# A small weight load moved from sixteen DMA engines to four

The last 64 rows of one weight matrix (72 KB of the 88.5 MB that the kernel loads) were loaded by all sixteen DMA engines. The change loads them by one transfer that only DMA engines 0 to 3 carry.

## The chip, the cores and the metric

One core of one Trainium2 chip. Times are device microseconds (us) of single executions, as medians of several. A ratio compares the fast runs of two kernels in the same rounds on the same chip and is given with its 95% interval, so it isn't quite the ratio of the medians. A run is fast when it lies within 1.5% of the fastest run of the same kernel. Landings and packet times come from one profiled execution of each kernel and are counted from the start of its span (the time from the first to the last instruction of the profile). The packet records carry no engine number: "engines 0 to 3" is the name of the four DMA engines that carried the four packets of x (a load of 4 rows). In profile lines PE is the matmul engine, PEld its weight loads, DVE, ACT and POOL are VectorE, ScalarE and GpSimd, SP is SyncE; a q behind a name marks what its sequencer does, such as issuing a load. L176 is line 176 of the kernel.

## The reference, cut to what matters

One decode step: attention over the last 2048 positions of a cache beside an MLP, both fed by a layer norm of x.

```python
xn = _layernorm(x)                       # x: 4 x 576
return x + _A_ref(xn, k_cache, v_cache, wq, wo) + _B_ref(xn, w1, w2, w3, w4)
...
def _B_ref(x, w1, w2, w3, w4):           # w1, w2: 576 x 576
    h = _gelu(_layernorm(x) @ w1)
    hs = shifted(h) @ w2                 # cut: four groups of columns, shifted
    x1 = x + hs
    return x1 + _gelu(_layernorm(x1) @ w3) @ w4
```

There are 4 rows of activations, so nearly all the work is to read the K and V windows and the weights once from memory.

## The kernel before

576 rows are 4 x 128 + 64. The first 512 rows of each weight go to 128 partitions. The 64 rows that are left (the "rag") are paired: one matrix takes the even partitions of a tile, another the odd ones, and the transposed activations hold zeros where the other matrix lies, so that one matmul over 128 partitions uses one of the two.

```python
def rag_pair(tile, even, odd):
    return [(tile[p:128:2, 0:w.shape[1]], w[512:576, :]) for p, w in enumerate((even, odd))]
...
ev_wq = [add_dma([(kt_t[:], A_wq[0:512, :]...)], "wq", (), -60),             # 4 MB
         add_dma(rag_pair(ragq3, B_w3, A_wq), "wqr", ["ragq3_zero"], -59)]
ev_r12 = add_dma(rag_pair(rag12, B_w1, B_w2), "r12", (), -58.5)             # the rag of w1 and w2
ev_w2 = add_dma([(w2main, ...)], "w2", (), -58)
ev_w1 = add_dma([(w1main, ...)], "w1", (), -57)
... # w3, sixteen K blocks of 2 MB, sixteen V blocks, wo, w4
def pe_h(h):
    def f(e):
        for r in range(4):
            e.matmul(HTps[h], lhsT=xn2T[:, r, :], rhs=w1main[:, r, ...], start=(r == 0), stop=False)
        return e.matmul(HTps[h], lhsT=xn2T[:, 4, :], rhs=rag12[:, ...], start=False, stop=True)
```

All loads but that of x are issued by SyncE on one queue, in this order.

## Time and profile before

| | before |
|---|---|
| time, median of 6 runs | 215.06 us (214.81 to 215.25) |
| span of the profiled execution | 213.7 us |
| loads of the kernel | 88.5 MB, 97.7% of the sixteen engines' span |
| last landing of a load | 211.48 us |
| that landing, engine by engine | spread over 2.15 us |

The first row is from the runs, the next two are from the page of the profile. The kernel is bound by its DMA engines (first packet 1.85 us, the DMA row at 9 in all slices between the first and the last). How the lines of this profile are read is shown in the prediction below.

### The profile page before, as it was taken

What the parts mean: (1) busy time and instruction counts of PE and PEld (TensorE: products, weight loads), DVE (VectorE), ACT (ScalarE), POOL (GpSimd) and SP (SyncE); (2) the same over time, 40 slices, a digit from 0 to 9 for tenths busy, and PEclk for the clock granted to TensorE, in tenths of its full rate; (3) what the DMA queues carried; (4) which work ended last, traced back from release to release, by engine and by line L of the source; (5) the groups of instructions that cost most, each with busy time, mean ns of one, the idle gap of its engine ahead of it and who ended that gap; (6) DMA issues with size and microseconds to landing.
All of it is one profiled execution on the core that took longest, in us unless ns stands there. A gap on an engine that the chain in (4) does not pass through costs nothing. (4 is left out here: it accounts for less than half of the span.)

```text
span 213.7 us, 5906 instructions
## 1 busy us (share of the span) xinstructions
PE 141.4 (66%) x2664; PEld 110.4 (52%) x2668; DVE 75.3 (35%) x147; ACT 61.2 (29%) x76; POOL 10.8 (5%) x38
## 2 busy tenths in 40 slices
PE   0038683999999999999996277133444433336995
PEld 0023363788878887888774067033434433334542
DVE  0142511477776676666664830100010001001000
ACT  2001032366655666666656620000000000000000
POOL 8300100000001000000000000000000000000000
PEclk9999999799999999999999655555555555555799
DMA  7999999999999999999999999999999999999993
GB/s 282 406 385 449 438 411 442 414 429 422 432 426 429 429 423 435 422 432 420 439 423 432 420 425 427 427 426 435 426 423 426 429 429 426 429 429 436 426 404 124
DMA packets 6690, 88.65 MB, mean 415 GB/s; under 512 B 780, under 2 KB 1048, under 8 KB 1560
## 3 DMA queue, kind: packets, MB, share of 16 engines
q1 hardware_dynamic: 6664, 88.50, 97.7%
q8 instruction: 8, 0.13, 0.2%
q14 instruction: 2, 0.02, 0.0%
q10 hardware_dynamic: 16, 0.01, 0.0%
HBM read 88.49 MB, written 0.00 MB: 414 GB/s over the span
## 5 line engine op out<-in xcount | busy, mean ns | idle before, releaser
L336 PE MATMUL ps<-perm_bf,ring 128*128 128x128 bf16 x1024 | 62.5, 221 | 3.0 <-PEq L575 2.4
L336 PEld LDWEIGHTS ps<-perm_bf,ring 128*128 128x128 bf16 x1024 | 58.3, 98 | 11.3 <-issue 11.1
L343 DVE COPY kt<-ps 128x1024 bf16<-128x1024 bf16 x80 | 52.4, 688 | 28.5 <-PE ps L336 28.0
L342 ACT ACTIVATE kt<-ps 128x1024 bf16<-128x1024 bf16 x48 | 48.4, 1023 | 33.0 <-PE ps L336 32.3
L417 PE MATMUL ps<-PTpad,ring 128*128 128x8 bf16 x1024 | 29.7, 168 | 41.5 <-PEq L575 37.5
L417 PEld LDWEIGHTS ps<-PTpad,ring 128*128 128x128 bf16 x1024 | 28.7, 104 | 42.6 <-issue 42.5
L552 ACT ACTIVATE out_sb<-ps 4x288 bf16<-4x288 f32 x1 | 0.4, 401 | 87.5 <-PE ps L434 87.5
L350 PE MATMUL ps<-kt,Qs 128*32 128x512 bf16 x272 | 18.5, 393 | 1.4 <-PEq L575 1.4
L406 DVE TENSOR_TENSOR PTpad<-PT,mU_bf 128x512 bf16<-128x512 bf16 x16 | 6.4, 421 | 29.7 <-PE ps L417 29.7
L429 DVE TENSOR_TENSOR OTn<-ps,rinvB 128x32 bf16<-128x32 f32 x4 | 0.8, 192 | 34.5 <-PE ps L417 34.5
L277 PE MATMUL ps<-ident_bf,xn_bf 4*128 4x4 bf16 x8 | 0.5, 170 | 13.9 <-DVE ragsrc L271 13.9
L350 PEld LDWEIGHTS ps<-kt,Qs 128*32 128x32 bf16 x272 | 5.9, 98 | 7.2 <-issue 2.2
L371 POOL COPY Qs<-Qpad 128x128 bf16<-128x128 bf16 x16 | 4.6, 293 | 86.8 <-PE ps L350 72.5
L277 PEld LDWEIGHTS ps<-ident_bf,xn_bf 4*128 4x128 bf16 x8 | 0.4, 111 | 14.0 <-issue 11.6
L434 PE MATMUL ps<-w,ORT 128*4 128x288 bf16 x64 | 5.8, 358 | 0.4 <-DVE ORT L456 0.4
L551 DVE CAST out_sb<-ps 4x288 bf16<-4x288 f32 x1 | 0.4, 446 | 14.5 <-PE ps L434 14.5
L434 PE MATMUL ps<-w,h2T_sb 128*4 128x288 bf16 x72 | 5.0, 286 | 0.4 <-DMA w<-in_B_w_dram 0.4
L264 ACT ACTIVATE sd<-mv 4x1 f32<-4x1 f32 x3 | 0.6, 202 | 15.8 <-DVE mv L262 15.8
L388 PE MATMUL ps<-kt,permT_bf 128*128 128x512 bf16 x3 | 1.8, 608 | 4.9 <-DVE kt L387 4.8
L434 PEld LDWEIGHTS ps<-w,ORT 128*4 128x4 bf16 x64 | 3.4, 106 | 3.0 <-DVE ORT L456 1.0
L434 PEld LDWEIGHTS ps<-w,h2T_sb 128*4 128x4 bf16 x72 | 2.9, 84 | 2.8 <-DMA w<-in_B_w_dram 1.8
L440 PE MATMUL ps<-zeros_bf 128*128 128x512 bf16 x13 | 3.8, 419 | 0.4 <-DVE OTn L429 0.2
(99 smaller groups left out, 65.9 us busy)
## 6 DMA issues: line engine op xcount, KB each, us to landing
ring<-in_A_k_cache_dram SPq DMA_DIRECT2D x16, 2048.0 KB, 14.4
ring<-in_A_v_cache_dram SPq DMA_DIRECT2D x16, 2048.0 KB, 17.4
w<-in_B_w_dram SPq DMA_DIRECT2D x2, 2304.0 KB, 21.9
w<-in_A_wo_dram SPq DMA_DIRECT2D x2, 2304.0 KB, 21.1
kt<-in_A_wq_dram SPq DMA_DIRECT2D x1, 4096.0 KB, 12.3
w<-in_B_w_dram SPq DMA_DIRECT2D x1, 2592.0 KB, 28.1
w<-in_B_w_dram SPq DMA_DIRECT2D x3, 576.0 KB, 13.6
w<-in_B_w_dram SPq DMA_DIRECT2D x1, 1296.0 KB, 30.7
```

Source lines behind the costliest of these rows:

```text
L277: e.transpose(XTps[idx][:, r, :], v[:, r, :], ident_bf[0:B, 0:B])
L336: ins = e.transpose(tb[n % 4][:, t, :], slot_t(c)[:, 8 * k + t, :], perm_bf[:])
L342: return "act", lambda e: e.activation(out=ktbuf[:, n % 16], in_=tb[n % 4], func=ACTF.Copy)
L343: return "dve", lambda e: e.tensor_copy(out=ktbuf[:, n % 16], in_=tb[n % 4])
L350: ins = e.matmul(Sps[32 * u:32 * u + 32, q, :].rearrange("p (t i) -> p t i", t=16), lhsT=Qs[:, c % NPOS, 32 * u:32 * u + 32], rhs=ktgrp[:, ...
L371: P(lambda e, c=c, cc=cc: e.tensor_copy(out=Qs[:, c % NPOS, :], in_=Qpad_t[:, 128 * cc:128 * cc + 128]), waits=["qT", "qs_zero"] + ([f"SC{ ...
L388: add("pe", lambda e, q=q: e.matmul(ps[:, 4 + q % 3, :], lhsT=permT_bf[:], rhs=PTx[:, q, :], start=True, stop=True), waits=[f"PTx{q}", "pe ...
L406: return lambda e: e.tensor_tensor(out=PTpad[:, c % 2], in0=PTv[:, :, cc, :].unsqueeze(2).to_broadcast([128, NT, NU, 2]), in1=mU_bf[:].uns ...
L417: ins = e.matmul(o_, lhsT=slot_t(c)[:, t, :], rhs=PTpad[:, c % 2, t].rearrange("p u e -> p (u e)"), start=(t == 0), stop=(t == NT - 1))
L429: add("dve", lambda e, hv=hv: e.tensor_tensor(out=hv(OTn), in0=OTps.rearrange("p (b h) -> p b h", b=B), in1=hv(rinvB), op=ALU.mult), waits ...
L434: return e.matmul(ACC[h], lhsT=lhsT, rhs=rhs, start=start, stop=stop, tile_position=(0, 32 * h), skip_group_check=True)
L440: ins = e.matmul(ps[:, 3, :], lhsT=zeros_bf[:, 0:128], rhs=zeros_bf[:, :], start=True, stop=True)
```

## The change

Intent: engines 0 to 3 finish early, so give them the whole of this load and take its share from the other twelve. The new transfer has outermost dimensions 16 (partitions) on one side and 4 (groups of rows) on the other. Four rows of w1 go side by side into one partition, so the rag becomes 16 partitions of 4 x 576 numbers, and its one matmul becomes four of 16 rows each.

```diff
+        w1rag = w4_t[0:16, 18 * D:22 * D]
...
+        P(lambda e: e.memset(rag12[:], 0.0), sig="rag12_zero", key=-98)
...
-        ev_r12 = add_dma(rag_pair(rag12, B_w1, B_w2), "r12", (), -58.5)
+        ev_r12 = add_dma([(w1rag, B_w1[512:576, :].rearrange("(b a c) n -> a b (c n)", b=4, a=4)),
+                          (rag12[1:128:2, :], B_w2[512:576, :])], "r12", ["rag12_zero"], -58.5)
...  # the columns of the normed x in the matching order (one copy)
+                for c in range(4):
+                    ins = e.transpose(XTps[idx][0:16, 4 + c, :], ragsrc[:, idx, 16 * c:16 * c + 16], ident_bf[0:B, 0:B])
...
-        add("dve", lambda e: e.tensor_copy(out=xn2T[:], in_=XTps[1]), ...)
+        add("dve", lambda e: e.tensor_copy(out=xn2T[:, 0:4, :], in_=XTps[1][:, 0:4, :]), ...)
+        add("dve", lambda e: e.tensor_copy(out=xn2T[0:16, 4:8, :], in_=XTps[1][0:16, 4:8, :]), ...)
...
-                return e.matmul(HTps[h], lhsT=xn2T[:, 4, :], rhs=rag12[:, ...], start=False, stop=True)
+                for c in range(4):
+                    ins = e.matmul(HTps[h], lhsT=xn2T[0:16, 4 + c, :], rhs=w1rag[:, ...], start=False, stop=(c == 3))
```

More of the change, by code (lines that the diff above doesn't have):

```diff
@@ L100, in bass_parallel_sum__sliding_block_cached__mixer_s_mlp__decode_kernel @@
         xnT = sb("xnT", [128, 5, 32], BF16)
-        xn2T = sb("xn2T", [128, 5, B], BF16)
+        xn2T = sb("xn2T", [128, 8, B], BF16)
         x1nT = sb("x1nT", [128, 5, 32], BF16)
@@ L146, in bass_parallel_sum__sliding_block_cached__mixer_s_mlp__decode_kernel @@
         HTps = [ps[0:B, 2 + k, 0:HALF] for k in range(2)]
-        XTps = [ps[:, k, a:a + 10].bitcast(BF16).rearrange("p (c b) -> p c b", b=B) for k, a in ((3, 300), (7, 0), (7, 12))]
+        XTps = [ps[:, k, a:a + 16].bitcast(BF16).rearrange("p (c b) -> p c b", b=B) for k, a in ((3, 300), (7, 0), (7, 20))]
         S = {}
@@ L269, in ln_ops @@
                                                  op0=ALU.subtract, op1=ALU.mult), waits=[f"{tag}_rstd"], sig=f"{tag}_n", key=k0 + 0.04)
-            odd = int(idx == 0)
-            add("dve", lambda e: e.tensor_copy(out=ragsrc[:, idx, odd:128:2], in_=dst[:, 512:D]), waits=[f"{tag}_n", "rag_zero"], sig=tag, key=k0 + 0.05)
+            r_out, r_in = ragsrc[:, idx, int(idx == 0):128:2], dst[:, 512:D]
+            if idx == 1:
+                r_out = ragsrc[:, idx, 0:64].rearrange("q (c a b) -> q c a b", c=4, a=4)
+                r_in = r_in.rearrange("q (b a c) -> q c a b", b=4, a=4)
+            add("dve", lambda e: e.tensor_copy(out=r_out, in_=r_in), waits=[f"{tag}_n", "rag_zero"], sig=tag, key=k0 + 0.05)
         def pe_xT(src, idx):
@@ L277, in f @@
                     e.transpose(XTps[idx][:, r, :], v[:, r, :], ident_bf[0:B, 0:B])
-                return e.transpose(XTps[idx][:, 4, :], ragsrc[:, idx, :], ident_bf[0:B, 0:B])
+                if idx != 1:
+                    return e.transpose(XTps[idx][:, 4, :], ragsrc[:, idx, :], ident_bf[0:B, 0:B])
+                for c in range(4):
+                    ins = e.transpose(XTps[idx][0:16, 4 + c, :], ragsrc[:, idx, 16 * c:16 * c + 16], ident_bf[0:B, 0:B])
+                return ins
             return f
@@ L283, in bass_parallel_sum__sliding_block_cached__mixer_s_mlp__decode_kernel @@
         add("pe", pe_xT(xn_bf, 0), waits=["ident_bf", "ln1"], sig="xT", key=-40)
-        add("dve", lambda e: e.tensor_copy(out=xnT[:, :, 0:B], in_=XTps[0]), waits=["xT", "xnT_zero"], sig="xnT", key=-39)
+        add("dve", lambda e: e.tensor_copy(out=xnT[:, :, 0:B], in_=XTps[0][:, 0:5, :]), waits=["xT", "xnT_zero"], sig="xnT", key=-39)
         def pe_q(r):
@@ L316, in bass_parallel_sum__sliding_block_cached__mixer_s_mlp__decode_kernel @@
         add("pe", pe_xT(xn2_bf, 1), waits=["ln2", "ident_bf"], sig="x2T", key=-36)
-        add("dve", lambda e: e.tensor_copy(out=xn2T[:], in_=XTps[1]), waits=["x2T"], sig="xn2T", key=-25)
+        add("dve", lambda e: e.tensor_copy(out=xn2T[:, 0:4, :], in_=XTps[1][:, 0:4, :]), waits=["x2T"], sig=None, key=-25)
+        add("dve", lambda e: e.tensor_copy(out=xn2T[0:16, 4:8, :], in_=XTps[1][0:16, 4:8, :]), waits=["x2T"], sig="xn2T", key=-24.9)
         def pe_zero(e):
@@ L474, in f @@
                     e.matmul(HTps[h], lhsT=xn2T[:, r, :], rhs=w1main[:, r, HALF * h:HALF * (h + 1)], start=(r == 0), stop=False)
-                return e.matmul(HTps[h], lhsT=xn2T[:, 4, :], rhs=rag12[:, HALF * h:HALF * (h + 1)], start=False, stop=True)
+                for c in range(4):
+                    ins = e.matmul(HTps[h], lhsT=xn2T[0:16, 4 + c, :], rhs=w1rag[:, c * D + HALF * h:c * D + HALF * (h + 1)], start=False, stop=(c == 3))
+                return ins
             return f
@@ L493, in bass_parallel_sum__sliding_block_cached__mixer_s_mlp__decode_kernel @@
         add("pe", pe_xT(x1n_bf, 2), waits=["ln3", "xn2T"], sig="x1T", key=-23)
-        add("dve", lambda e: e.tensor_copy(out=x1nT[:, :, 0:B], in_=XTps[2]), waits=["x1T", "x1nT_zero"], sig="x1nT", key=-23)
+        add("dve", lambda e: e.tensor_copy(out=x1nT[:, :, 0:B], in_=XTps[2][:, 0:5, :]), waits=["x1T", "x1nT_zero"], sig="x1nT", key=-23)
         for h in range(2):
```

## The prediction

The sum came to 215.03 - 0.19 + 0 + 0 = 214.84 us, raised to 214.87 us for the first rival. The -0.19 us rests on the changed transfer being carried by four engines, the same that carried x.

> **What bounds the kernel now.** I read the page's table of 40 slices first, then its table of queues, then the chain that ended last in order of time, then the timeline of the first 37 us, and last the trace's records of single DMA packets and semaphore updates, which no view prints and which I therefore give in words.
>
> The table of 40 slices (one slice is 5.34 us):
>
> ```profile
> PE   0038683999999999999996277133444433336995
> DMA  7999999999999999999999999999999999999993
> GB/s 282 406 385 449 438 411 442 414 429 422 432 426 429 429 423 435 422 432 420 439 423 432 420 425 427 427 426 435 426 423 426 429 429 426 429 429 436 426 404 124
> ```
>
> The DMA row is at 9 from the second slice to the 39th, at some 427 GB/s, while PE is idle for long stretches after slice 22. The kernel loads 88.5 MB, so 88.5 MB / 427 GB/s = 207 us of its 213.7 us span is the sixteen DMA engines working without a break. The rest is the start (first packet 1.85 us after the span's start) and a tail. The queue table says the same, and shows one thing more:
>
> ```profile
> q1 hardware_dynamic: 6664, 88.50, 97.7%
> q8 instruction: 8, 0.13, 0.2%
> ```
>
> Queue 1 holds the kernel's own loads. Queue 8 holds eight fetches of instructions, 16 KB each, which ride on the same engines.
>
> The chain that ended last, in order of time (start us, us, what):
>
> ```profile
> 178.16 32.29 DMA w<-in_B_w_dram
> 210.45 0.04 issue
> 210.49 1.36 PE ps L434 x18
> 211.86 0.43 DVE out_sb L551
> ```
>
> The end hangs on the landing of the last w4 transfers at 210.45 us; 3.25 us of matmul, copy and store follow. So what counts is when the slowest of the sixteen engines has delivered its last packet. The last transfer's semaphore gets sixteen updates, one for each engine. Counted from the first, they come at 0, 0.18, 0.20, 0.22, 0.26, 0.45, 0.58, 0.99, 1.41, 1.70, 1.71, 1.76, 1.84, 1.91, 2.12 and 2.15 us. The engines are thus uneven by 2.15 us at the end although each carries the same bytes. The trace shows why: until 29 us the spread is only 0.60 us in the large transfers, and then one engine at a time falls back by about 1.53 us (a gap of 1.00 to 1.08 us in its packets and a slower packet after it), each time at the start of a 16 KB instruction fetch. Seven such steps are visible, on seven different engines; the eighth fetch starts at 209.1 us and shows no step. Two 8 KB fetches, at 48.3 and 87.9 us, push one engine each back by 0.97 and 0.67 us.
>
> [...]the load of x, with 4 rows, made four packets of 1152 B and five updates of its semaphore. [...]a 1152 B packet took 51 ns, a 4608 B packet 178 ns, a 16384 B packet 611 ns (the next starts 4 ns before the end), so 24.5, 26.5 and 27.0 bytes/ns.
>
> **The change, part by part.**
>
> *DMA.* Before, the last 64 rows of w1 are 64 packets of 1152 B, 4 on each engine: 4 x (51 - 4) = 188 ns, and 9 - 4 = 5 ns for the semaphore packet, 193 ns for every engine. After, they are 16 packets of 4608 B, 4 on each of engines 0 to 3: 4 x (178 - 4) + 5 = 701 ns there, nothing on the other twelve. So engines 0 to 3 gain 701 - 193 = 508 ns of work and engines 4 to 15 lose 193 ns. In all, 4 x 508 - 12 x 193 = -284 ns of engine time, 18 ns on the mean: as a saving of work this is nothing. It is a shift of load, worth -0.19 us if the slowest engine is one of 4 to 15 and no engine of 0 to 3 overtakes it, and up to +0.51 us if the slowest is one of 0 to 3.
>
> *Which engines are slow?* The packet records carry no engine number, but the four packets of x mark engines 0 to 3. Each engine's phase against the others is nearly constant between fetches (sixteen offsets 0, 163, ... 543, 561, 569 ns recur within 10 ns after every large transfer), so I followed the four: at 23 us they stand at 306, about 337 (one of three at 337 to 340), 470 and 543 ns. The one at 470 takes the 8 KB fetch at 48.3 us and ends at about 1.41 us of the list above. The one at 543 takes no fetch that I can see and ends at about 0.56. The one at 306 is either untouched (0.26) or takes the second 8 KB fetch (0.99). The one near 337 is open: two of its group of three take a 16 KB fetch and end at about 1.75 and 1.91, the third does not. So none of engines 0 to 3 is for certain among the seven with a 16 KB fetch, and one may be. That somebody chose engines 0 to 3 speaks for their being early. Then after the change the four end at up to 1.41 + 0.51 = 1.92, 0.56 + 0.51 = 1.07 and 0.99 + 0.51 = 1.50 us, the other twelve at up to 2.15 - 0.19 = 1.96. The last landing moves by -0.19 us.
>
> *Start.* One more GpSimd fill of 128x576 (some 0.5 us, from the 128x512 fill of 0.52) stands before the fills of xnT and ragsrc and before the issue of the small transfers. Timeline lines (start us, us, what):
>
> ```profile
> 2.25 0.23 POOL L199 MEMSET xnT<- 128x160 bf16 x1
> 2.41 0.41 POOL L197 MEMSET ragsrc<- 4x384 bf16 x1
> 2.62 3.33 SPq L176 DMA_DIRECT2D w<-in_B_w_dram  x6
> 11.27 0.19 DVE L271 COPY ragsrc<-xn_bf 4x64 bf16<-4x64 bf16 x1
> ```
>
> The first reader of ragsrc runs at 11.27 us, and the queue in front of the six transfers is the 4 MB of wq, some 10 us. A delay of 0.5 us in either is free.
>
> *PE and DVE.* The transposes of the rag columns become four instead of one, the rag matmuls of w1 eight instead of two, the copy of xn2T two instead of one.
>
> ```profile
> 23.65 0.15 DVE L317 COPY xn2T<-ps 128x20 bf16<-128x20 bf16 x1
> 23.94 0.65 PE L474 MATMUL ps<-w,xn2T 128*4 128x288 bf16 x4 [0.70 <-DVE xn2T L317]
> 24.43 0.29 PE L475 MATMUL ps<-w,xn2T 128*4 128x288 bf16 x1
> 25.95 0.29 PE L277 MATMUL ps<-ident_bf,x1n_bf 4*128 4x4 bf16 x4 [0.62 <-DVE ragsrc L271]
> 36.27 0.97 PE L336 MATMUL ps<-perm_bf,ring 128*128 128x128 bf16 x14 [2.44 <-PEq L575]
> ```
>
> Four matmuls took from 23.94 to 24.43 us, 0.122 us each; six more are 0.73 us. Three more transposes are about 0.1 us, one more copy 0.15 us. Against that, PE waits 0.62 us before L277, and 2.44 us at 36.27 us for the first K block, whose last engine lands at 35.98 us. The 1.0 us is taken up by these two waits; the K loop starts when the data is there. After that no instruction differs.
>
> *Sum.* 215.03 - 0.19 + 0 + 0 = 214.84 us; I write 214.87 for the chance of the first rival.
>
> **The rivals.**
>
> 1. *A slow engine is among 0 to 3.* For it: one of the four could not be told from two that take a 16 KB fetch (by count alone, 2 of 3). Against: all fetches that I could place on single engines missed the other three but for an 8 KB one, and the design. If so, that engine ends at 1.75 + 0.51 = 2.26 or 1.91 + 0.51 = 2.42 instead of 2.15: +0.1 to +0.3 us, 215.15 to 215.3. In the worst case (the very last one) +0.51, 215.54.
> 2. *The fetches move.* The added instructions shift the code, so a fetch may come at another time, on another engine, or once more. One step of 1.53 us on an engine that is late already, less the 0.19, would add about 1.3 us: 216.4. Against: some 20 instructions more, and so far each fetch falls on an engine that had none. A luckier split can also gain: the mean of the sixteen finishing times is 1.09 us, so perfect balance would give 2.15 - 1.09 = 1.06 us, 213.97. No balance can do more.
> 3. *The PE prologue becomes the bound.* It would have to outgrow 2.44 us with 1.0; and even a late K loop must first drain a queue that holds three transfers (issue to landing 14.4 us against about 4.9 us for one transfer). Worth 0.
> 4. *The transfer is hidden anyway* and the spread of single runs (214.92 to 215.2) covers everything: 215.0.
>
> **Range and chances.** The main theory and the fourth rival give 214.8 to 215.0, the first 215.15 to 215.54; the second alone leaves this band. I put 65% on the first engine-balance reading, 25% on the first rival and 10% on the second. That gives a range of 214.6 to 215.4. A change of 2% is 4.3 us; perfect balance gains 1.06 and two unlucky steps lose 3, so nothing here reaches it: same 0.98.
>
> **What would show it.** Right: the r12 load made of 16 packets of 4608 B and 64 of 1152 B; the last w4 landing about 0.2 us earlier; the last semaphore's spread at about 1.9 to 2.0 us; PE still waiting, about 1.5 to 2.4 us, for the first K block; the DMA row unchanged. Wrong: a last engine that stands 0.1 us or more behind the others while the twelve moved forward (first rival); another number of 16 KB fetches, or a step in the last 20 us (second); no wait of PE before the first K block (third). A change above 1.06 us in the good direction would break the whole picture.

## The result, and the profile after

The changed kernel took 214.90 us in the median of 6 runs (214.70 to 215.01), the kernel before 215.06 us. The ratio is 0.9992, with an interval of 0.9979 to 1.0005. Five more rounds gave 0.9995 (0.9981 to 1.0008). The forecast was 214.87 us. The timing alone does not resolve the difference: both intervals contain 1. What follows rests on the traces.

The table of 40 slices of the changed kernel:

```profile
PE   0048864999999999999996178033434433336985
DMA  7999999999999999999999999999999999999993
GB/s 289 400 389 436 435 437 417 430 431 421 417 433 439 421 424 436 428 421 427 439 424 421 436 429 424 424 433 430 421 430 430 427 424 433 430 425 443 425 404 130
```

The DMA row is the same, digit for digit: the engines still work without a break, and the kernel still hangs on them. The table of queues:

```profile
q1 hardware_dynamic: 6604, 88.50, 97.8%
q8 instruction: 8, 0.13, 0.2%
```

Queue 1 has 60 packets less than before (6664). That is the change itself: 64 packets became 16 (48 less), and 4 engines instead of 16 report the end of the transfer (12 less). There are still eight 16 KB fetches of instructions. The chain that ended last (start us, us, what):

```profile
177.98 32.23 DMA w<-in_B_w_dram
210.22 0.04 issue
210.26 1.40 PE ps L445 x18
211.66 0.43 DVE out_sb L564
```

Each of its steps stands about 0.2 us earlier than before (210.22 against 210.45 us, 211.66 against 211.86 us), and none is longer by more than 0.04 us. Semaphore updates of the last load, engine by engine, in us after the first of the sixteen:

```
before        0 .18 .20 .22 .26 .45 .58 .99 1.41 1.70 1.71 1.76 1.84 1.91 2.12 2.15   last at 211.48, mean at 210.43
changed       0 .14 .19 .28 .29 .65 .88 1.39 1.60 1.61 1.64 1.67 1.68 1.81 1.89 2.06  last at 211.28, mean at 210.34
```

The last landing moved by -0.20 us. Only about half of it (0.11) is a smaller distance of the last engine from the mean, 1.06 to 0.95 us. The mean moved by -0.09 us, of which 0.05 was already there when the first load (wq) had landed, before any changed transfer; that is a difference of the start, not of the change.

The confinement can be seen at work in the changed kernel's trace: at the w2 load that follows, twelve engines finish within 0.40 us of the first, and four stand apart at 0.66, 0.72, 0.86 and 0.90 us. These are engines 0 to 3, which carried the four packets of 178 ns each in between, 0.70 us more. Followed to the end, they finish at 0.65, 0.88, 1.39 and 1.89 us of the list above; two of them fall back by 0.7 and about 1.0 us at the 8 KB fetches on the way. The seven that meet a 16 KB fetch are all among the other twelve.

The prologue of the changed kernel (timeline; start us, us, what, and in brackets the idle time before it):

```profile
2.24 0.58 POOL L197 MEMSET w<- 128x576 bf16 x1
2.85 3.46 SPq L177 DMA_DIRECT2D w<-in_B_w_dram  x6
2.93 0.41 POOL L199 MEMSET ragsrc<- 4x384 bf16 x1
11.11 0.19 DVE L277 COPY ragsrc<-xn_bf 4x64 bf16<-4x64 bf16 x1
21.67 0.14 DVE L328 COPY xn2T<-ps 16x16 bf16<-16x16 bf16 x1
22.54 0.65 PE L487 MATMUL ps<-w,xn2T 16*4 16x288 bf16 x4
31.09 1.51 PE L527 MATMUL ps<-w,x1nT 128*32 128x387 bf16 x36 [1.45 <-DMA w<-in_B_w_dram]
36.23 0.94 PE L347 MATMUL ps<-perm_bf,ring 128*128 128x128 bf16 x14 [1.53 <-PEq L588]
```

The fill took 0.58 us and pushed the six issues from 2.62 to 2.85 us; the first reader of ragsrc came long after. The four small matmuls (16 rows) took as long as four large ones (128 rows), 0.65 us. PE still waits 1.53 us before the K loop, and it enters that loop at 36.23 us, where it was 36.27 us before. The added work is hidden.

### The profile page after: what moved, and what is told of

Same layout as the page of the kernel before. It is cut to its first block, busy times and chain, and to the rows that moved or that the text cites. A ratio compares the mean times of both kernels' runs of the same rounds, so it can differ in the third digit from the quotient of the medians.

```text
span 213.5 us, 5926 instructions
## 1 busy us (share of the span) xinstructions
PE 140.4 (66%) x2673; PEld 109.4 (51%) x2677; DVE 75.2 (35%) x148; ACT 61.9 (29%) x76; POOL 11.4 (5%) x39
## 5 line engine op out<-in xcount | busy, mean ns | idle before, releaser
L347 PEld LDWEIGHTS ps<-perm_bf,ring 128*128 128x128 bf16 x1024 | 57.5, 98 | 11.9 <-issue 11.9
L353 ACT ACTIVATE kt<-ps 128x1024 bf16<-128x1024 bf16 x48 | 49.1, 1023 | 31.6 <-PE ps L347 30.2
L361 PE MATMUL ps<-kt,Qs 128*32 128x512 bf16 x272 | 17.8, 382 | 1.4 <-PEq L588 1.4
L527 PE MATMUL ps<-w,x1nT 128*32 128x387 bf16 (+6 forms) x90 | 5.1, 356 | 1.8 <-DMA w<-in_B_w_dram 1.5
L527 PEld LDWEIGHTS ps<-w,x1nT 128*32 128x32 bf16 x90 | 3.9, 113 | 3.2 <-DMA w<-in_B_w_dram 2.0
L445 PE MATMUL ps<-w,ORT 128*4 128x288 bf16 x64 | 4.8, 317 | 0.4 <-DVE ORT L467 0.4
```

Of the source, the lines that this page charges most:

```text
L347: ins = e.transpose(tb[n % 4][:, t, :], slot_t(c)[:, 8 * k + t, :], perm_bf[:])
L353: return "act", lambda e: e.activation(out=ktbuf[:, n % 16], in_=tb[n % 4], func=ACTF.Copy)
L361: ins = e.matmul(Sps[32 * u:32 * u + 32, q, :].rearrange("p (t i) -> p t i", t=16), lhsT=Qs[:, c % NPOS, 32 * u:32 * u + 32], rhs=ktgrp[:, ...
L445: return e.matmul(ACC[h], lhsT=lhsT, rhs=rhs, start=start, stop=stop, tile_position=(0, 32 * h), skip_group_check=True)
L527: ins = e.matmul(H2ps[k][32 * g:32 * g + 32, :].rearrange("p (x c) -> p x c", c=9)[:, :, off:off + cnt], lhsT=x_, rhs=w[:, base_:base_ + 1 ...
```

## The experiments

Theories. **Load shift**: the end is set by the slowest engine; that is one of number 4 or higher; the change takes 193 ns from it. Rivals: a slow engine among 0 to 3; a gain from other parts of the change or from fewer packets; mere noise. All runs gave correct results. (One execution of the kernel before took 244.91 us at a granted clock of 0.624; it stood in the rounds of the rest, the confinement alone and the confined load twice and three times, is slow and is not used.) The kernel before ran anew beside each set of runs: its median was 214.94 us beside the markers, "changed, again" and the new layout on 16 engines, 215.06 us beside the four runs just named, and 215.04 us beside the last copy and the old load once more. So the ratios count, and medians of different rows differ by up to 0.12 us for that alone. Landings from one trace of each:

| run | median us | ratio to before (95%) | mean of 16 engines' last landing | last engine |
|---|---|---|---|---|
| before | 215.06 | | 210.43 | 211.48 |
| changed | 214.90 | 0.9992 (0.9979 to 1.0005) | 210.34 | 211.28 |
| changed, again | 214.90 | 0.9995 (0.9981 to 1.0008) | 210.37 | 211.31 |
| the rest without the transfer | 215.08 | 1.0001 (0.9987 to 1.0015) | 210.42 | 211.44 |
| old load once more, on all 16 | 215.19 | 1.0006 (0.9992 to 1.0019) | 210.58 | 211.41 |
| confined load twice | 215.62 | 1.0020 (1.0006 to 1.0034) | 210.58 | 212.06 |
| confined load three times | 216.12 | 1.0051 (1.0036 to 1.0065) | 210.74 | 212.93 |
| confinement alone | 215.17 | 1.0005 (0.9991 to 1.0019) | 210.80 | 211.52 |
| new layout on 16 engines | 215.64 | 1.0029 (1.0015 to 1.0043) | 211.18 | 212.12 |
| confined twice, second copy elsewhere | 216.06 | 1.0052 (1.0039 to 1.0066) | 211.19 | 212.43 |

### Which engine is which: markers

Both kernels with fifteen tiny loads queued behind the last w4 load.

```diff
+        for k in range(1, 16):
+            ev_m = add_dma([(mark[0:k, 32 * k - 32:32 * k], B_w1[0:k, 0:32])], ("m", k), (), KT + 15 + 0.1 * k)
```

> The kernel before, plus 15 tiny loads queued behind the last w4 load, of 1, 2, ... 15 partitions[...]; the number of marker packets then names each engine in the trace. Load-shift theory: the engines that end last (more than 1.6 us behind the first) are all of number 4 or higher; engines 0 to 3 end at least 0.7 us before the last one. Rival (a slow engine among 0 to 3): at least one of them is within 0.5 us of the last. Both: time as before within 0.2 us, because the markers come after the last w4 packet of each engine.

> The changed kernel with the same 15 markers. Load-shift theory: engines 0 to 3 end 0.70 us later against the others than in the kernel before, none of them is the last, and the last engine is one that had a 16 KB instruction fetch; eight such fetches, seven steps, none on engines 0 to 3. Rival: one of 0 to 3 is the last, by 0.1 us or more. Time as the changed kernel within 0.2 us.

The k-th marker had exactly k engine updates, for every k from 1 to 15, so the sets of engines could be taken apart one by one: the engine numbers are names, in the order in which the markers, from one row up, add an engine. In the kernel before, engines 2, 0, 1 and 3 finished the last w4 load 0.00, 0.26, 1.06 and 1.31 us after the first; the last engine finished at 2.01 us. Seven engines finished at 1.72 us or later, and all have number 5 or higher. So none of engines 0 to 3 had the step of a 16 KB fetch; engines 1 and 3 show the smaller one of the 8 KB fetches. This is shown for one trace. In the changed kernel, engines 0, 2, 1 and 3 finished at 1.00, 1.15, 1.83 and 2.27 us, and the latest of the others at 2.27 as well; the two differ by 5 ns, and the markers do not tell which of them was the very last. No step of a 16 KB fetch fell on engines 0 to 3 here either. From the one trace to the other the four moved by +0.56 us on the mean and the twelve by -0.30 us, so they shifted against each other by 0.86 us where 0.70 was expected; that fits the first four of the markers being the four that carry the changed transfer. That "none of them is the last" was expected with room to spare, so this is half a miss, and it tells something: the shift uses up all the room that engine 3 has. The time was a miss too: 215.45 and 215.26 us in single runs, 0.5 and 0.4 us above the unmarked kernels, while their spans were 213.8 and 214.0 us; so these two runs serve as identification only.

### The changed kernel again

> The changed kernel once more, to narrow the ratio. Load-shift theory: 0.9991 of the kernel before (0.19 us less), interval not reaching 1.0003. Rival (the transfer is hidden anyway, all is noise): 1.0000, interval on both sides of it.

0.9995, interval 0.9981 to 1.0008 (medians 214.90 us, and 214.94 us for the kernel before in the same rounds). The sign agrees, the interval is too wide to tell the two apart. The last landing was at 211.31 us, again before the 211.48 us of the kernel before.

### The rest without the transfer

The kernel before, with one more fill, three more transposes, six more matmuls of zeros, and one more copy; loads as they were.

```diff
+                for _ in range(3):
+                    e.matmul(HTps[h], lhsT=zeros_bf[0:16, 0:B], rhs=zeros_bf[0:16, 0:HALF], start=False, stop=False)
```

> Everything but the transfer: the kernel before with the one more fill and the wait for it, three more transposes, six more matmuls of 16 rows (of zeros, so the result is unchanged) and one more copy, its loads untouched. Load-shift theory: as before within 0.05 us, ratio 1.0000, because this lies in waits of PE. Rival (code, its fetches or the start gave the gain): 0.9992 as the changed kernel. Second rival (they cost time that the balance first has to earn back): 1.001 or more.

1.0001 and a last landing at 211.44 us: as before within 0.05 us, as the load-shift theory has it. Engines started 0.11 us earlier on average here than in the kernel before (2.02 against 2.13 us, the mean of the first packets), but that was gone when wq had landed (on the mean of the engines at 12.84 against 12.83 us). So this run says nothing on the 0.05 us that the changed kernel was ahead at that landing.

### The confined load twice, and three times

```diff
-                          (rag12[1:128:2, :], B_w2[512:576, :])], "r12", ["rag12_zero"], -58.5)
+                          (rag12[1:128:2, :], B_w2[512:576, :]),
+                          (w4_t[0:16, 22 * D:26 * D], B_w1[512:576, :].rearrange("(b a c) n -> a b (c n)", b=4, a=4))], "r12", ["rag12_zero"], -58.5)
```

> The changed kernel with the confined load made twice, the second copy to unused columns: 701 ns more on engines 0 to 3, nothing on the others. In the traces of the changed kernel the latest of engines 0 to 3 stands 0 to 0.2 us ahead of the last engine. Load-shift theory: the last landing moves by 0.50 to 0.70 us, 215.4 to 215.6 us, ratio to before 1.0017 to 1.0025. Rival (the twelve set the end with room to spare, or no single engine's load shows in the time): at most the mean, 4 x 701 / 16 = 0.18 us, ratio 1.000.

> The same with the confined load made three times: 1402 ns more on engines 0 to 3 than in the changed kernel. Load-shift theory: 0.70 us more than with the load made twice, since engines 0 to 3 are by then the last: 216.1 to 216.3 us, ratio to before 1.005 to 1.006. Rival (mean load): 0.35 us over the changed kernel, ratio 1.0008.

The chain's DMA step of the first (load made twice), then of the second (three times):

```profile
178.75 32.24 DMA w<-in_B_w_dram
```

```profile
179.66 32.20 DMA w<-in_B_w_dram
```

They end at 210.99 and 211.86 us, against 210.22 us in the changed kernel (as there, this is the third last w4 load; the last one landed at 212.06 and 212.93 us, against 211.28 us). The times were 215.62 and 216.12 us, ratios 1.0020 and 1.0051. In the first of the two the last landing moved by 0.78 us where 0.50 to 0.70 was expected. Both ratios lie in the expected ranges of the load-shift theory and clear of the mean-load rival (0.18 and 0.35 us). The second step is 0.50 us in the medians and 0.87 us in the two traces where 0.70 was expected. The single runs spread by 0.49 and 0.63 us here, more than the 0.31 us of the changed kernel; why was not looked into. In the second trace one engine stands 0.79 us behind the next, and the kernel waits for it: here a single engine's load sets the time of the whole kernel.

### The old load once more, on all sixteen

```diff
+                          (w4_t[0:128:2, 26 * D:27 * D], B_w1[512:576, :])], "r12", ["rag12_zero"], -58.5)
```

> The changed kernel with another 64 packets of 1152 B spread over all 16 engines, to unused columns (the shape of the old load): 193 ns more on every engine. Load-shift theory: the gain is given back, 0.19 us over the changed kernel, 215.1 us, ratio to before 0.9999 to 1.0004; packets stay at 51 and 178 ns. Rival (that the confined layout itself saves time, whatever the twelve carry): the ratio stays at 0.9992 to 0.9995.

1.0006 and 215.19 us, 0.15 us over the kernel before in the same rounds. The ratio is a little above the expected range, which its interval (0.9992 to 1.0019) covers, and the interval covers the rival's 0.9992 to 0.9995 too. The packets stayed at 51 and 178 ns. The last landing came at 211.41 us, 0.12 us after that of the changed kernel. So it agrees in sign and rough size and proves little more.

### The confinement alone, and the new layout on sixteen engines

Two attempts to cut the change in half, and both went against the expectation. The first keeps the 64 half-used partitions and only reorders the rows so that the source has an outermost 4; the second keeps the new layout but lets sixteen engines carry it. The packets on queue 1 show how many carried each: the first had 6652, 12 less than the kernel before (4 reports of the end instead of 16), the second 6616, 12 more than the changed kernel (16 instead of 4).

```diff
# confinement alone (against before)
-                rag_pair(rag12, B_w1, B_w2)
+                [(rag12[0:128:2, :], B_w1[512:576, :].rearrange("(b a) n -> a b n", a=4)),
+                 (rag12[1:128:2, :], B_w2[512:576, :])]
# new layout on sixteen (against the changed kernel)
-                (w1rag, B_w1[512:576, :].rearrange("(b a c) n -> a b (c n)", b=4, a=4))
+                (w1rag, B_w1[512:576, :].rearrange("(p c) n -> p (c n)", c=4))
```

> The confinement alone: the kernel before, but the 64 rows of w1 keep their 64 packets of 1152 B to every second partition, in an order of rows that gives the source an outermost 4 (two access patterns of one copy change to match). Engines 0 to 3 gain 12 x 47 = 564 ns, the others lose 193 ns. In the marker run of the kernel before, engines 0 to 3 ended 0.7 us or more ahead of the last, so after this they end at up to 1.31 + 0.56 = 1.87 us and the other twelve at up to 2.01 - 0.19 = 1.82. Load-shift theory: 0.13 to 0.19 us less than before (ratio 0.9992). Rival (other parts of the change, or fewer packets, gave the gain): 1.0000.

> The changed kernel with everything but the confinement: the same 16 packets of 4608 B to partitions 0 to 15, the same fill, transposes, copies and matmuls, but rows grouped by 4 in their own order, so that both sides have an outermost 16 and every engine carries one packet (179 ns against 193 ns before). Load-shift theory: the gain is gone, within 0.05 us of the kernel before (ratio 0.9998), 0.17 us over the changed kernel. Rival (fewer small packets, or the other parts of the change, are what helped): the same time as the changed kernel, ratio 0.9992.

Ratios 1.0005 and 1.0029 where 0.9992 and 0.9998 were expected. Neither theory had this. The stretch from 15 to 17.6 us, in which these small loads run (us, then busy time of PE, PEld, DVE, ACT and POOL, the PE clock, the DMA share, GB/s), for the kernel before, for the confinement alone, and for the new layout on sixteen:

```profile
15.00:17.60 2.60, 2.60 (x32) 1.00 (x28) 0.00 (x0) 0.00 (x0) 0.00 (x0) 1.00 1.04 418
```

```profile
15.00:17.60 2.60, 2.60 (x28) 0.95 (x24) 0.00 (x0) 0.00 (x0) 0.00 (x0) 1.00 1.02 370
```

```profile
15.00:17.60 2.60, 2.60 (x32) 1.02 (x28) 0.00 (x0) 0.00 (x0) 0.00 (x0) 1.00 1.01 324
```

The engines are as busy as before (share 1.0) but move less (370 and 324 GB/s instead of 418): their packets take longer. In the kernel before and in the changed kernel, every packet of 1152 B in this stretch takes 51 ns and every one of 4608 B takes 178 ns. From 14 to 20.5 us, in the confinement alone 175 of 256 packets of 4608 B took over 181 ns, up to 251, and in the new layout on sixteen 169 of 272, up to 547 ns. Summed over all packets of that time the excess is 4.6 and 9.1 us of engine time, which is 0.29 and 0.57 us on each of sixteen engines, most of the 0.37 and 0.75 us by which the mean landing moved. That the engines got in each other's way is the reading to be tested: in the new layout sixteen engines write to 16 partitions, and in the confinement alone four engines write to partitions of a range that the loads of 128 partitions beside them write as well.

The next run tests whether the target partitions matter. (HBM, in the expectation below, is the memory that the loads read.)

### The second copy to other partitions

As the confined load made twice, with one edit:

```diff
-                          (w4_t[0:16, 22 * D:26 * D], ...
+                          (w4_t[64:80, 22 * D:26 * D], ...
```

> As the run with the confined load made twice (ratio 1.0020), but the second copy goes to partitions 64 to 79 instead of 0 to 15: same source, same 16 packets, same engines 0 to 3. [...]packets of 4608 B take over 178 ns, engine time over the base is 2 us or more in sum, and the run is 0.3 to 0.7 us slower than the second copy to partitions 0 to 15 (ratio 1.0035 to 1.005). Rival (reading of HBM, or the order of the rows, made those packets slow): packets at 178 ns, ratio 1.0020.

Ratio 1.0052, just above the expected range, against 1.0020 (intervals 1.0039 to 1.0066 and 1.0006 to 1.0034, each against the kernel before in its own rounds). The same stretch with the second copy at partitions 0 to 15, then at 64 to 79:

```profile
15.00:17.60 2.60, 2.21 (x32) 0.67 (x20) 0.34 (x1) 0.34 (x1) 0.00 (x0) 1.00 1.02 415
```

```profile
15.00:17.60 2.60, 2.60 (x32) 0.94 (x24) 0.00 (x0) 0.00 (x0) 0.00 (x0) 1.00 1.03 340
```

Same source, same packets, and again four engines (6624 packets on queue 1, 20 more than in the changed kernel: 16 and four reports of the end). With the other target 145 of 288 packets took over 181 ns, up to 360, with 8.9 us of excess in sum; with partitions 0 to 15 none did. Between these two runs it is therefore the target partitions that decide, not the reading and not the order of rows; for the confinement alone and the new layout the same cause is inferred. What the transfers share at those partitions was not shown, and which engine writes which partition was not measured.

## Why the prediction was right or wrong

The time was forecast at 214.87 us and measured at 214.90 us, inside the range, and "within 2%" was right. By its steps:

- **Bound by the slowest engine's last packet.** Right. Load added on four engines appears in the time far above its mean over sixteen (for the second copy the ratios to the kernel before, 1.0020 against 0.9992 and 0.9995, make 0.5 to 0.6 us, where the mean would be 0.18).
- **-284 ns of work, 508 ns more on four engines, 193 ns less on twelve.** Right in kind: 16 packets at 178 ns each, and the four engines stand apart in the trace. The packet count fell by 60, as this layout makes it.
- **No slow engine among 0 to 3.** Right, and now by number: 0.00, 0.26, 1.06 and 1.31 us against 2.01 us for the last. Where each stood was left open for two of them; in the marker run two are early and two carry the 8 KB fetches. That fits the ends that were given, 0.56 us for an engine without a fetch and 1.41 us for one with the first 8 KB fetch, but it is another execution and can't check them one by one.
- **The last landing moves by -0.19 us.** The trace shows -0.20 us, but that agreement is partly luck. The imbalance fell by 0.11 us, and the rest was the mean. In the marker pair the last landing moved by only -0.08 us (211.48 to 211.40), and the imbalance did not fall at all (0.96 us both times): engine 3 drew level with the last, and the last of the other twelve came no more than 0.09 us earlier itself, although their mean moved by -0.30 us. The term was at its upper bound: I took the other twelve to stay last, at 2.15 - 0.19 = 1.96 us, with the four at up to 1.92 us, and a difference of 0.04 us is less than what changes from one execution to the next (the spread of the last load was 2.06, 2.15 and 2.27 us in three traces of the changed kernel).
- **The fetches move.** They did, without harm: the first came at 28.4 us instead of 30.3 us, an eighth was still the last, at 209.0 us, and there were still eight. That the added code is what moved them was not shown.
- **Prologue hidden.** Right: 1.53 us of wait left where 1.5 to 2.4 were named, K loop entered at 36.23 us; and the rest without the transfer took 1.0001 of the time before.
- **One line was misread.** The 210.45 us in the chain is the landing of the third last w4 load, not of the last, so 2.2 us and not 3.25 us follow the last landing. No term of the sum rests on it.
- **Not foreseen.** The prediction treats the partitions that a transfer writes as indifferent. For this change it made no difference, because its packets stayed at 51 and 178 ns. For its two nearest relatives slower packets cost 0.29 and 0.57 us for every engine, more than the 0.19 us that this balance was to give.

So the trace shows the shift of load that was meant. How much more could be shifted was not run: the doubled load adds work to the four and takes none from the twelve. But with engine 3 level with the last of the twelve in the marker run, a larger share for it would make it the last. That the changed kernel is faster than the kernel before by about 0.1 us is likely (0.9992, 0.9995, and last landings at 211.28, 211.31 and 211.40 us in its three traces against 211.48 us in both of the kernel before) but not settled by these timings.

## What to carry to other kernels

In a kernel that keeps its DMA engines busy throughout, look at the finishing time of each engine, not at the mean share: here the end belonged to the slowest (a second copy of the load on four engines cost 0.5 to 0.6 us, where its mean over sixteen is 0.18), and the bound on any rebalancing was the last engine's distance from the mean (1.06 us of 215). When a transfer is confined to few engines, choose the partitions that it writes with care, and read the packet durations to see whether they stay short: here partitions 64 to 79 instead of 0 to 15 made 145 of 288 packets longer. Before asking for a gain of 0.2 us, ask whether it can be told from the noise: here the eleven rounds of the changed kernel could not do it.
